# Attention and two MLPs on one core: the row maxima negated two slots at a time, the exponentials one slot later

## The chip, the core and the metric

The kernel runs on one core of a Trainium2 chip. The metric is the time of one execution on the device in microseconds (us). Before the change three runs give a median of 1149.24 us (1142.69 to 1151.27).

The engines that matter here are TensorE (PE, matmuls; PEld is its weight loading), VectorE (DVE), ScalarE (ACT), GpSimd (POOL) and SyncE (SP), which issues the DMAs. Each runs its own instructions in the order of the program, and waits for the others through semaphores.

## The reference

Softmax attention over 4 batches and 12 heads (448 positions, 64 dimensions), with q and k normalized by their root mean square, then two MLPs on 1792 tokens:

```python
q_n, k_n = (rmsnorm(q, g_q), rmsnorm(k, g_k))
scores = scale * np.matmul(q_n, k_n.transpose(0, 1, 3, 2))
scores = scores - np.max(scores, axis=-1, keepdims=True)
attn = np.exp(scores)
attn = attn / (np.sum(attn, axis=-1, keepdims=True) + 1e-09)
attn_out = np.matmul(attn, v)
...
a = x @ w1
b = x @ w2
h = a * b @ w3
x = h @ w_out
...
h = x @ w_in
g = h * np.clip(h + 3.0, 0.0, 6.0) / 6.0
out = g @ w_out
```

## The kernel before

Two heads form a pair, and there are 24 pairs. A pair's scores are made in 8 slots of 112 queries: slot s of pair i is head s // 4, query block s % 4. The main loop of `attention` counts slots t from 0 to 192 and some more. In slot t it emits, in this order:

- `score`: two matmuls (L627, L628) of 112x448 scores into a PSUM bank of the tag "s", of which there are two;
- `expo` of slot t - 1: ACT takes the exponential of the slot in place, with the negated row maximum as its bias, and sums the row (L646; the sum is a second, short ACT instruction);
- `trans` of a pair that began LG = 8 slots earlier: four PE transposes (L653) into a bank of the tag "t", one 128-key block kb of the pair each slot, 7 blocks in 8 slots. Block kb = 0 needs slots 0 to 3 of its pair, block 3 all eight;
- `tlo` of the block of one slot before: DVE takes the low part `xl` (L672);
- `scale_max`: one DVE instruction scales the scores out of the bank into `PP` and takes the row maximum (L634; the maximum comes out through a second, short DVE instruction). Its column of the tile `mx` is column s;
- `negate`: DVE writes minus that maximum to column 8 + s of `mx` (L641), one element per partition;
- `thi`: ACT takes the high part `xh` (L662) of this slot's block, and `pv` multiplies blocks with V (L701, L705, L706, and L687, L693, L696);
- `fill`: work of the first MLP (L252, L391, L396, L88 to L90) with its weight preparation (L148, L149, L151, L338, L340), so that PE has matmuls between the steps of attention;
- tasks that are due in the slot: loads, the splitting of q, k and v into high and low parts (L594, L600, L606, L608, L615, L616), the statistics of q and k (L510, L518, L523 to L553), and the row sums' end (L725, L726), which is due in slot t = 8i + 9 of pair i.

`anchors[t]` keeps the slot's last score matmul, its maximum and the exponential that is emitted in slot t + 1. Filling work of slot t is emitted so that it stands behind the anchors of slot t - 2 or t - 3 on its engine, and some tasks behind those of t - 1 and t.

What stands on each engine is settled by the tile framework's scheduler, which takes the emitted order as priority and puts an instruction ahead of another where its operands come earlier by its own estimate. A changed instruction can therefore move others, on every engine. POOL works in this stage on six kinds of instruction, all with operands in SBUF: the low parts of k, v and x, the low parts of two kinds of weights, and the division by the row sums.

The stage of attention with the first MLP as its filler lasts from about 20 to 600 us. Behind it only matmuls of the second MLP and their weights' preparation run.

## Time and profile before

| | |
|---|---|
| runs, median (lowest to highest) | 1149.24 us (1142.69 to 1151.27) |
| the profiled execution's own time; its span | 1141.81 us; 1140.0 us |
| PE busy | 1103.1 us (97%) |
| DVE busy | 850.8 us (75%), 1927 instructions |
| ACT busy | 812.4 us (71%), 1729 instructions |
| POOL busy | 177.9 us (16%), none of it behind 640 us |
| DMA queue of SP | 76.2% of 16 engines' span |
| granted clock of TensorE, mean | 0.998 |

A busy time is a share of the span and not yet a reason for its length: an engine that is idle costs something only where the engine that sets the end waits for it. So the waits of PE, and the chain of work that ended last, are read beside the busy times.

### The profile page before, as it was taken

The page shows a single profiled execution, that of the slowest core. Times are in us where ns is not written, and L with a number is a line of the kernel's source. Part 1 is how long each engine was busy: PE and PEld are TensorE (multiplying, and loading weights), DVE is VectorE, ACT ScalarE, POOL GpSimd, SP SyncE. Part 2 cuts the span into 40 slices and gives each one's busy share as a digit, 9 for nine tenths or more (in the row PEclk, how much of TensorE's full clock was granted, in tenths as well). Part 3 has the DMA queues.
Part 4 walks back from the last instruction along what each step waited for, and adds up shares of the span by engine and source line. Part 5 has one row for each costly group of instructions (what it writes and reads, how often), then busy time and mean ns, then how long its engine had stood idle before and what let it go on. Part 6 is the DMA issues. An engine that isn't in the chain of part 4 may idle for free.

```text
span 1140.0 us, 17361 instructions
## 1 busy us (share of the span) xinstructions
PE 1103.1 (97%) x5483; PEld 944.0 (83%) x5483; DVE 850.8 (75%) x1927; ACT 812.4 (71%) x1729; POOL 177.9 (16%) x156
## 2 busy tenths in 40 slices
PE   5999999999999999999999999999999999999998
PEld 3545666788887888888888899899989989999998
DVE  5757988779866888778753225999988998887764
ACT  6989778899758878787754433766666776666764
POOL 1133223554322213221102000000000000000000
PEclk9999999999999999999999999999999999999999
DMA  8999655689889988997789998665469955434972
GB/s 267 331 317 342 213 171 164 243 293 377 272 279 316 308 295 269 336 342 253 232 287 324 382 362 299 217 214 200 164 228 362 389 172 168 153 117 160 335 264 74
DMA packets 109660, 299.04 MB, mean 262 GB/s; under 512 B 13280, under 2 KB 46048, under 8 KB 109568
## 3 DMA queue, kind: packets, MB, share of 16 engines
q1 hardware_dynamic: 109568, 297.93, 76.2%
q8 instruction: 43, 0.70, 0.3%
q14 instruction: 49, 0.40, 0.1%
HBM read 230.61 MB, written 67.27 MB: 261 GB/s over the span
## 4 chain that ended last, share of the span: by engine, by line
PE 60%; ACT 7%; DMA 7%; DVE 3%; issue 2%; POOL 0%; SPq 0%; ACTq 0%; POOLq 0%; DVEq 0%
PE acc L1304 17%; PE bank L391 10%; PE sB L1242 8%; PE sA L1242 8%; PE bank L396 5%; DMA rsb<-rsd 2%; PE bank L653 2%; ACT PP L646 1%; PE bank L88 1%; PE bank L89 1%; PE bank L90 1%; PE bank L627 1%; PE bank L628 1%; PE bank L706 1%; DMA raw<-in_wo_dram 1%
## 5 line engine op out<-in xcount | busy, mean ns | idle before, releaser
L1304 PE MATMUL acc<-g,wt 128*128 128x448 f32 x1008 | 211.7, 366 | 1.2 <-ACT g L1192 1.0
L1304 PEld LDWEIGHTS acc<-g,wt 128*128 128x128 f32 x1008 | 188.9, 188 | 17.7 <-ACT g L1192 1.9
L391 PE MATMUL bank<-xhl,ws 128*128 128x448 f32 x768 | 180.5, 367 | 1.6 <-ACT bs L367 1.3
L391 PEld LDWEIGHTS bank<-xhl,ws 128*128 128x128 f32 x768 | 143.5, 188 | 15.1 <-ACT bs L367 1.8
L634 DVE CUSTOM_DVE_ANT_0 PP<-bank,rb,rq 112x448 f32<-112x448 f32 x192 | 128.7, 675 | 27.4 <-PE bank L628 21.1
L646 ACT ACTIVATE PP<-PP,mx 112x448 f32<-112x448 f32 x192 | 127.5, 665 | 28.1 <-DVE mx L641 24.3
L1242 PE MATMUL sA<-xo,wt 128*128 128x448 f32 x504 | 112.0, 366 | 1.1 <-ACT u L1253 1.1
L1242 PE MATMUL sB<-xo,wt 128*128 128x448 f32 x504 | 112.2, 367 | 0.8 <-ACT u L1253 0.6
L252 PE MATMUL bank<-woh,w 128*128 128x384 f32 x256 | 97.6, 509 | 14.6 <-DVE woh L151 10.9
L1242 PEld LDWEIGHTS sB<-xo,wt 128*128 128x128 f32 x504 | 94.4, 188 | 9.9 <-ACT u L1253 1.9
L1242 PEld LDWEIGHTS sA<-xo,wt 128*128 128x128 f32 x504 | 94.6, 188 | 9.6 <-ACT u L1253 1.5
L662 ACT ACTIVATE xh<-bank 128x448 fp32r<-128x448 f32 (+1 forms) x156 | 83.1, 539 | 24.6 <-PE bank L653 20.5
L653 PEld LDWEIGHTS bank<-ident,PP 112*128 112x128 f32 x672 | 78.8, 141 | 23.9 <-issue 6.1
L1011 DVE TENSOR_TENSOR wt<-wf,wt 128x384 fp32r<-128x384 f32 x160 | 87.3, 555 | 15.1 <-ACT wt L1010 14.9
L672 DVE TENSOR_TENSOR xl<-bank,xh 128x448 fp32r<-128x448 f32 x142 | 87.4, 617 | 11.5 <-ACT xh L662 10.1
L653 PE MATMUL bank<-ident,PP 112*128 112x112 f32 x672 | 94.1, 261 | 1.5 <-DVE xl L672 1.1
L396 PE MATMUL bank<-xhl,ws 128*128 128x448 f32 x384 | 94.5, 366 | 0.0
L252 PEld LDWEIGHTS bank<-woh,w 128*128 128x128 f32 x256 | 48.9, 196 | 43.7 <-DVE woh L151 13.4
L148 ACT ACTIVATE raw<-raw 128x384 f32<-128x384 f32 (+1 forms) x112 | 63.8, 569 | 28.6 <-DMA raw<-in_wo_dram 11.6
L1010 ACT ACTIVATE wt<-wf 128x384 fp32r<-128x384 f32 x160 | 80.4, 517 | 4.8 <-PE acc L1304 2.7
L151 DVE SCALAR_TENSOR_TENSOR raw<-raw 128x384 int32<-128x384 int32 x80 | 48.9, 613 | 46.0 <-ACT raw L149 38.8
L627 PE MATMUL bank<-K,Q 128*112 128x448 f32 x192 | 77.7, 407 | 1.5 <-DVE mx L634 1.4
(134 smaller groups left out, 2110.3 us busy)
## 6 DMA issues: line engine op xcount, KB each, us to landing
ws<-w12d SPq DMA_DIRECT2D x48, 768.0 KB, 6.2
ws<-wpd SPq DMA_DIRECT2D x32, 768.0 KB, 6.5
wf<-wfd SPq DMA_DIRECT2D x56, 384.0 KB, 5.6
raw<-in_wo_dram SPq DMA_DIRECT2D x44, 384.0 KB, 5.8
td<-G SPq DMA_DIRECT2D x32, 448.0 KB, 2.5
G<-td SPq DMA_DIRECT2D x32, 448.0 KB, 6.2
raw<-in_w_dram SPq DMA_DIRECT2D x32, 384.0 KB, 6.9
w12d<-ws SPq DMA_DIRECT2D x16, 768.0 KB, 5.9
```

Source lines behind the costliest of these rows:

```text
L252: nc.tensor.matmul(ps[:, :NH], W["w3"][a, c // 4][:, cs], W["woh"][c, n], start=c == 0, stop=c == M1 - 1)
L391: nc.tensor.matmul(ps[:, :S], w[:, 0, ks], x[:, y, :], start=k == 0 and y == 0, stop=False)
L396: nc.tensor.matmul(ps[:, :S], w[:, 1, ks], L["xhl"][i][:, 0, :], start=False, stop=k == KD - 1)
L627: nc.tensor.matmul(ps[:CP, :S], qs, k1[:, j, :], start=True, stop=False)
L634: anchors[8 * i + s].append(nc.vector.tensor_tensor_reduce(out=T["PP", i][:, c, sl], in0=ps[:CP, :S], in1=T["rb", i][:, sl], op0=ALU.mult, ...
L646: anchors[8 * i + s].append(nc.scalar.activation(v, v, AF.Exp, bias=T["m", i][:, 8 + s : 9 + s], accum_out=T["sum", i][:, s : s + 1]))
L653: nc.tensor.transpose(ps[:, c * CP : c * CP + CP], src[:, c, kb * P : kb * P + P], ident[:CP, :CP])
L662: nc.scalar.activation(hi, ps, AF.Copy)
L672: nc.vector.tensor_sub(lo, ps, hi)
L1011: nc.vector.tensor_sub(t[:, 1, :], src, t[:, 0, :])
L1242: mm = nc.tensor.matmul(ps[:, :S], w[:, a, ks], x[:, c, :], start=first and k == 0 and n == 0, stop=k == KD // 2 - 1 and n == 2, skip_grou ...
L1304: nc.tensor.matmul(ps, w[:, y, ns], x[:, z, :], start=first and a == 0, stop=end and a == 2, skip_group_check=h in "674")
```

## The change

The negation is made in every other slot, for two columns of `mx` at once: in an odd slot s it reads columns s - 1 and s and writes columns 7 + s and 8 + s. The exponential of a slot is emitted two slots behind its score instead of one. It is kept in the same place of `anchors` as the exponential that was emitted in that slot before, so the filling work stays behind the exponential of the same loop step. The last exponential is emitted in slot 193 instead of 192.

```diff
@@ score
-            anchors[8 * i + s] = [nc.tensor.matmul(ps[:CP, :S], qs, k2[:, j, :], start=False, stop=True)]
+            anchors.setdefault(8 * i + s, []).append(nc.tensor.matmul(ps[:CP, :S], qs, k2[:, j, :], start=False, stop=True))
@@ negate
-            nc.vector.tensor_scalar_mul(m[:, 8 + s : 9 + s], m[:, s : s + 1], -1.0)
+            nc.vector.tensor_scalar_mul(m[:, 7 + s : 9 + s], m[:, s - 1 : s + 1], -1.0)
@@ expo
-            anchors[8 * i + s].append(nc.scalar.activation(
+            anchors.setdefault(8 * i + s + 1, []).append(nc.scalar.activation(
                 v, v, AF.Exp, bias=T["m", i][:, 8 + s : 9 + s], accum_out=T["sum", i][:, s : s + 1]))
@@ the loop over slots
-            if 0 < t <= 8 * NP:
-                expo(*divmod(t - 1, 8))
+            if 1 < t <= 8 * NP + 1:
+                expo(*divmod(t - 2, 8))
...
-                negate(*divmod(t, 8))
+                if t % 2:
+                    negate(*divmod(t, 8))
```

On DVE, slots 4 and 5 of pair 11 (L634 is a slot's maximum and its short second instruction, L641 the negation, L672 a low part) stood so before:

```order
L634 ISA PP,mx<-bank,rb,rq 112x448
L634 ISA mx 112x1
L672 TENSOR_TENSOR xl<-bank,xh 128x448
L641 TENSOR_SCALAR mx<-mx 112x1
L634 ISA PP,mx<-bank,rb,rq 112x448
L634 ISA mx 112x1
L641 TENSOR_SCALAR mx<-mx 112x1
```

With the change the same two slots stand so (L721 is an addition for an earlier pair):

```order
L634 ISA PP,mx<-bank,rb,rq 112x448
L634 ISA mx 112x1
L721 TENSOR_TENSOR xs<-bank,xs 64x448
L634 ISA PP,mx<-bank,rb,rq 112x448
L634 ISA mx 112x1
L641 TENSOR_SCALAR mx<-mx 112x2
```

The first slot's negation is gone from between the two maxima, and one instruction of two columns stands behind the second maximum.

On ACT, the exponentials of slots 4 to 7 of the same pair (L646) stood so among the copies (L662 is a high part `xh`):

```order
L646 ACTIVATE PP,sum<-PP,mx 112x448
L510 ACTIVATE nat<-nat 112x1024
L646 ACTIVATE PP,sum<-PP,mx 112x448
L662 ACTIVATE xh<-bank 128x448 x2
L606 ACTIVATE K<-kr 128x896
L594 ACTIVATE Q<-qr,gs 128x896
L646 ACTIVATE PP,sum<-PP,mx 112x448
L359 ACTIVATE xhl<-xs 128x448 x2
L372 ACTIVATE abh<-bs 128x448
L646 ACTIVATE PP,sum<-PP,mx 112x448
```

With the change they stand in two pairs:

```order
L646 ACTIVATE PP,sum<-PP,mx 112x448 x2
L662 ACTIVATE xh<-bank 128x448
L372 ACTIVATE abh<-bs 128x448
L606 ACTIVATE K<-kr 128x896
L594 ACTIVATE Q<-qr,gs 128x896
L662 ACTIVATE xh<-bank 128x448
L646 ACTIVATE PP,sum<-PP,mx 112x448 x2
```

Over the whole program 38 of the 191 steps from one exponential to the next had nothing between them on ACT before, and 86 have nothing between them now. DVE has 96 instructions fewer; the counts on the other engines are the same, their order is not.

## Rows read from the trace of the kernel before

**Rows 1.** Windows: busy us (and instructions) by engine, granted clock, DMA share, GB/s.

```profile
core 0: us, PE busy (x) PEld busy (x) DVE busy (x) ACT busy (x) POOL busy (x), PEclk, DMA share, GB/s
20.00:100.00 80.00, 76.25 (x303) 43.48 (x302) 51.88 (x148) 72.58 (x160) 21.22 (x19) 1.00 0.97 321
100.00:220.00 120.00, 115.50 (x555) 83.38 (x554) 102.42 (x273) 100.24 (x227) 45.13 (x39) 1.00 0.63 202
220.00:300.00 80.00, 79.04 (x419) 67.75 (x418) 65.33 (x160) 71.49 (x159) 36.84 (x32) 1.00 0.95 332
300.00:380.00 80.00, 77.19 (x415) 68.06 (x414) 57.47 (x158) 56.28 (x126) 19.13 (x17) 0.98 0.87 290
380.00:580.00 200.00, 196.87 (x1078) 174.79 (x1078) 160.97 (x424) 159.96 (x358) 46.93 (x38) 1.00 0.87 289
```

**Rows 2.** Waits of PE, 20 to 580 us: us in total, times, longest.

```profile
PE bank L705 <- ACT xh L662: 3.5, 5, 1.3
PE bank L696 <- DVE xh L674: 2.4, 1, 2.4
PE bank L252 <- DVE woh L151: 1.5, 1, 1.5
PE bank L252 <- DVE wst L245: 1.5, 1, 1.5
PE bank L627 <- DVE mx L634: 1.4, 4, 0.6
PE bank L391 <- ACT bs L367: 1.3, 1, 1.3
PE bank L653 <- DVE xl L672: 1.1, 5, 0.3
```

**Rows 3.** The page: the chain that ended last, shares of the span by engine.

```profile
PE 60%; ACT 7%; DMA 7%; DVE 3%; issue 2%; POOL 0%; SPq 0%; ACTq 0%; POOLq 0%; DVEq 0%
```

**Rows 4.** The negation's line: duration ns lowest/median/highest; who waited for it.

```profile
L641 DVE TENSOR_SCALAR mx<-mx x192: 130/146/156, 27.4 to 574.1; 112x1 f32<-112x1 f32 x192
  ACT PP L646: 24.3, 27
```

**Rows 5.** Timeline of DVE near 311 us: start us, duration us, instruction.

```profile
311.10 0.15 DVE L641 TENSOR_SCALAR mx<-mx 112x1 f32<-112x1 f32 x1
311.17 0.17 DVE L523 TENSOR_SCALAR ss<-ss 112x32 f32<-112x32 f32 x1
...
312.99 0.14 DVE L641 TENSOR_SCALAR mx<-mx 112x1 f32<-112x1 f32 x1
313.05 0.61 DVE L672 TENSOR_TENSOR xl<-bank,xh 128x448 fp32r<-128x448 f32 x1
```

**Rows 6.** The row sums' line: duration ns lowest/median/highest; below, its group on DVE.

```profile
L725 DVE TENSOR_SCALAR sum<-sum x24: 158/172/1133, 40.4 to 577.5; 112x8 f32<-112x8 f32 x24
L725 DVE TENSOR_SCALAR sum<-sum 112x8 f32<-112x8 f32 x24 | 10.0, 416 | 8.3 <-ACT PP L646 8.1
```

**Rows 7.** Timelines of DVE and of POOL around the longest L725.

```profile
297.88 1.13 DVE L725 TENSOR_SCALAR sum<-sum 112x8 f32<-112x8 f32 x1
299.05 0.20 DVE L726 RECIPROCAL sum<-sum 112x8 f32<-112x8 f32 x1
...
297.42 2.67 POOL L360 TENSOR_TENSOR xhl<-xs,xhl 128x448 fp32r<-128x448 f32 x2
```

**Rows 8.** Timelines of DVE and of POOL around a negation.

```profile
101.69 0.14 DVE L641 TENSOR_SCALAR mx<-mx 112x1 f32<-112x1 f32 x1
101.75 0.61 DVE L672 TENSOR_TENSOR xl<-bank,xh 128x448 fp32r<-128x448 f32 x1
...
100.90 1.10 POOL L227 TENSOR_TENSOR ws<-raw,ws 128x384 fp32r<-128x384 f32 x1 [0.26 <-ACT ws L225]
```

**Rows 9.** Groups of POOL, 20 to 580 us: busy us, mean ns; idle before.

```profile
L608 POOL TENSOR_TENSOR K<-kr,K 128x448 fp32r<-128x448 f32 x48 | 56.2, 1193 | 92.2 <-ACT K L606 84.8 <-PE bank L653 7.3
L340 POOL TENSOR_TENSOR ws<-raw,ws 128x384 fp32r<-128x384 f32 x22 | 23.2, 1063 | 22.7 <-ACT ws L338 19.2 <-DMA w12d<-ws 3.5
```

**Rows 10.** Groups of ACT, 20 to 580 us.

```profile
L646 ACT ACTIVATE PP<-PP,mx 112x448 f32<-112x448 f32 x192 | 127.5, 665 | 28.1 <-DVE mx L641 24.3 <-PE bank L396 2.2 <-PE bank L561 0.9
L662 ACT ACTIVATE xh<-bank 128x448 fp32r<-128x448 f32 (+1 forms) x148 | 78.9, 539 | 24.6 <-PE bank L653 20.5 <-PE bank L561 2.9
L646 ACT ACTIVATION_READ_ACCUMULATOR PP<-PP,mx 112x1 f32 x192 | 37.2, 194 | 0.0
```

## The prediction

> **What bounds the kernel now.** I read the windows first, because the change touches one stage alone. From 20 to 580 us PE is busy 76.25 + 115.50 + 79.04 + 77.19 + 196.87 = 544.85 of 560 us [rows 1]: it is idle for 15.2 us. DVE is busy there 51.88 + 102.42 + 65.33 + 57.47 + 160.97 = 438.1 us (78%), ACT 460.6 us (82%). So PE sets the end, and DVE and ACT matter where PE waits for them. The waits of PE come next [rows 2]: those that DVE ended among the rows shown are 2.4 + 1.5 + 1.5 + 1.4 + 1.1 = 7.9 us, those that ACT ended 3.5 + 1.3 = 4.8 us. That is 12.7 us which quicker DVE and ACT could give back; the rest of the span is matmuls that nobody removes. Third, the chain of work that ended last [rows 3]: DVE holds 3% of it, some 34 of 1140 us against 850.8 us that it is busy, so about 4% of a microsecond of DVE work reaches the end; ACT holds 7%, some 80 us of 812.4, about 10%. I use these two shares as the price of a microsecond on either engine.
>
> **The change part by part.** *96 negations go.* Each lasts 0.146 us [rows 4], but DVE starts its next instruction 0.06 to 0.07 us after the negation's start [rows 5]. So DVE gains 96 x 0.06 = 5.8 us; the other bound is the whole duration, 96 x 0.146 = 14.0 us. I take 5.8, because the next start is what the next instruction sees.
>
> *96 negations become two columns wide.* The nearest wider row of the same operation is L725 with 8 columns, at least 0.158 us [rows 6]: at most 0.012 us each, 1.2 us; at least nothing. I take 1.2.
>
> *The wider form may wait for POOL.* The negation of one column never lasts over 0.156 us, in 192 instances, POOL at work or not [rows 4]: at 101.69 us it lies inside a POOL instruction (100.90 to 102.00) and takes 0.14 [rows 8]. L725 is the same kind of DVE instruction with 8 columns, from SBUF to SBUF: its median is 0.172 us and its longest 1.133, and its mean 0.416 [rows 6]. The longest starts at 297.88, when POOL has been at work for 0.46 us, and ends at 299.01; POOL's two instructions from 297.42 take 2.67 us, so the first ends near 298.8 to 298.9 [rows 7]. It stood until POOL's first instruction was over. Two columns could behave as one, or as eight. If as eight: POOL is busy for 21.22 + 45.13 + 36.84 + 19.13 + 46.93 = 169.3 of the 560 us, 30% [rows 1], and its instructions last about 1.2 us [rows 9], so 96 x 0.30 = 29 negations meet one and wait for half of it, 0.6 us: 17.4 us. The bounds are nothing (as one column), and 96 times L725's mean over its median, 96 x (0.416 - 0.172) = 23.4 us. I take 17.4: the operation, its memory and its type are L725's, and only one column has been seen to be exempt.
>
> The Trainium skill speaks against the change here: *Vector Engine (DVE) Microarchitecture Reference*, section 5.1 (performance modes), says that a one-source instruction on two elements per partition in SBUF runs in the mode that uses both ports, and *SBUF — State Buffer*, "Who interferes with whom", that such an instruction and a GpSimd one exclude each other, whichever starts first holding the ports for all of its time. By that rule the 17.4 us stand; by the rows of the one-column form alone they would be 0. That two elements are enough is shown by no row of before.
>
> What is queued behind such a wait is DVE's next instruction, mostly a maximum (L634) or a low part (L672). For these wait PE's next scores (1.4 us in 4 waits now) and transposes (1.1 us in 5) [rows 2], and the two exponentials on ACT wait for the negation itself.
>
> DVE in sum: -5.8 + 1.2 + 17.4 = +12.8 us. At 4% that is +0.5 us at the end.
>
> *The exponentials move a slot.* Each issues two ACT instructions, 0.665 and 0.194 us, and no DMA [rows 10]. ACT now idles 24.3 us, 27 times, for the negation [rows 4]. An odd slot's exponential now has its bias ready one slot earlier; an even one waits for the pair's negation, which its slot's successor makes, as close behind as before. So I let half of that idle time go: -12.2 us of ACT, at 10% -1.2 us. What is late next is what stands behind two adjacent exponentials: 86 - 38 = 48 more adjacent pairs in the order push a following copy by 0.665 us. PE waited 5 times among 148 copies `xh` [rows 2, 10], 3.4%: 48 x 0.034 x 0.665 = +1.1 us.
>
> *The row sums (L725) come due in slot 9 of their pair; the exponential of slot 7 now is emitted in that slot instead of the one before.* DVE waits 8.1 us for these exponentials now [rows 6]. If it doubles, DVE loses 8 us, at 4% +0.3 us. The bound is 24 x (0.665 + 0.194) = 20.6 us, +0.8. The transposes of key block 3 need that exponential in slot 11; two slots of cover remain, at some 2.9 us a slot (560 us for 192). Were the cover gone, ACT's 0.86 us would stand in front of PE 24 times, 20.6 us.
>
> *The order of the other instructions moves on every engine, SP's loads among them.* No row prices that. The instructions and bytes are the same; between 20 and 100 us the DMA share is 0.97 [rows 1], where a load that is issued later can't be caught up. I take 0, with a few us both ways.
>
> **The sum.** +0.5 - 1.2 + 1.1 + 0.3 = +0.7 us on the profiled execution's 1141.8: 1142.5. That execution lies 7.4 us below the median 1149.24 and just below the lowest run shown, 1142.69. The runs of a changed kernel may fall at either level, so I choose the middle and add half of the 7.4: **1146 us**.
>
> **The rivals.**
>
> *Slower: the POOL waits sit in PE's path.* Place: DVE's queue between a pair's second maximum and the next score bank. For it: L725 shows waits of up to 0.97 us over its median, and the scores already wait for maxima [rows 2, 6]. Against it: DVE has 122 idle us in the stretch to absorb them [rows 1], and PE has filling matmuls between scores. If all 29 waits reach PE, +17.4 us: 1159 on the profiled scale, 1163 on the forecast's. It decides slower by over 1% from about 20 of the 29 on (20 x 0.6 = 12 us). The two sections of the Trainium skill named above state the rule behind this rival.
>
> *Faster: two columns don't wait for POOL, and the pairs free ACT.* Then DVE gains 4.6 to 14.0 us, ACT 12.2 us or more, and the waits of PE shrink: at most the 12.7 us of rows 2, so 1129 on the profiled scale and 1133 on the forecast's. For it: half the biases are ready early. Against it: it needs nearly all of PE's waits gone, one of which (2.4 us, L696) has nothing to do with maxima.
>
> *Nothing but the order's shuffle.* The negations' time and waits stay off PE's path entirely, and only the new order shows, +/- 6 us: 1140 to 1152. For it: PE is 97% busy over 560 us. Against it: the change pairs the exponentials all through the stage, which the shuffle alone would not.
>
> **How the numbers follow.** Forecast 0.50, slower 0.19, faster 0.15, shuffle alone 0.16. One per cent is 11.5 us, and about what a measurement of this kernel can tell from no change (its three runs spread 8.6 us). Forecast and shuffle lie within it: 0.66. The range leaves out about one in ten at each end: low 1134, at nearly the faster rival's 1133, and high 1160, some way into the slower one. The likeliest case's own range is 1140 to 1152.
>
> **What the profile after would show.** Line L641: 96 instances; if the POOL term is right, its median stays near 0.15 us and its longest is near 1 us, its mean near 0.3; if it stays below 0.17 throughout, that term is nothing. L646's wait for L641 falls from 24.3 to near 12 us. L725's wait for L646 rises to near 16 us. PE's waits for `xh` rise by about a microsecond, and PE's idle time from 20 to 580 us stays between 12 and 20 us. The prediction is wrong if PE's idle time grows past 25 us with waits on L634 or L641 in front (the slower rival), if it falls below 6 (the faster one), or if PE waits for a load that it did not wait for before.

## The result, and the profile after

The changed kernel takes 1159.3 us (median of 12 runs, 1154.38 to 1166.84), the kernel before beside it 1144.66 us (12 runs, 1140.87 to 1153.41). The ratio is 1.0122, with a 95% interval of [1.0097, 1.0147]: slower by 1.2%, some 14 us (the medians differ by 14.6). The forecast was 1146 us, and that the change would stay within 1% either way. The time lies inside the range of 1134 to 1160 us, at its upper end; that the kernel would not get slower was wrong.

The profiled execution of the changed kernel took 1162.23 us (before: 1141.81), so the two traces differ by more than the medians, 20.5 us of span. The stages after the change, which answer to [rows 1] (columns: busy us and instructions by engine, granted clock of TensorE, DMA share, GB/s):

```profile
core 0: us, PE busy (x) PEld busy (x) DVE busy (x) ACT busy (x) POOL busy (x), PEclk, DMA share, GB/s
20.00:100.00 80.00, 75.35 (x286) 42.09 (x285) 51.21 (x126) 69.59 (x154) 21.13 (x18) 0.96 0.92 304
100.00:220.00 120.00, 113.88 (x524) 80.65 (x523) 101.85 (x250) 97.18 (x220) 40.23 (x35) 0.97 0.64 208
220.00:300.00 80.00, 79.50 (x418) 70.00 (x419) 62.59 (x141) 68.62 (x156) 36.18 (x32) 0.98 0.87 300
300.00:380.00 80.00, 76.86 (x408) 66.41 (x407) 55.69 (x136) 57.06 (x129) 23.04 (x19) 0.98 0.91 294
380.00:580.00 200.00, 190.18 (x1022) 166.79 (x1021) 164.55 (x376) 152.88 (x340) 46.51 (x38) 0.98 0.85 281
```

Two things are to be seen. PE is busy for 535.8 of the 560 us, so it is idle for 24.2 us instead of 15.2. And the granted clock is below 1.00 in every stage, where before it was so in one. In these stages PE does 112 matmuls fewer (2658 against the 2770 of [rows 1], where a matmul at a border counts in both rows); they are left for the time after 580 us.

The mean granted clock of the whole span, before and after (columns: span, clock):

```profile
core 0: 1140.0 us, clock 0.998
```

```profile
core 0: 1160.5 us, clock 0.988
```

A clock of 0.988 over 1160.5 us is 13.9 us of full-speed time not granted, one of 0.998 over 1140.0 us 2.3 us. So the two traces differ by 11.6 us for the clock and by 9.1 us for PE's idle time between 20 and 580 us. Together that is 20.7, and the spans differ by 20.5. The whole span agrees: the same 5483 matmuls keep PE busy for 1115.3 us instead of 1103.1, 12.2 us longer, and PE is idle for 45.2 us instead of 36.9.

These are two single executions, and a pair that lies far apart. Each run on record carries its granted clock. Over the 12 runs of the change it is 0.985 to 0.994, on average 10.3 us of full-speed time not granted; over the 125 runs of the kernel before that were taken beside the experiments it is 0.991 to 1.000, on average 3.7 us. So the clock stands for some 6.6 of the 14 us, about half, and PE's idle time for about the other half.

The waits of PE from 20 to 580 us after the change, which answer to [rows 2] (columns: us in total, times, longest):

```profile
PE bank L705 <- ACT xh L662: 7.2, 7, 1.9
PE bank L627 <- DVE mx L634: 4.3, 8, 1.2
PE bank L696 <- DVE xh L674: 3.5, 3, 1.8
PE bank L391 <- ACT bs L367: 2.5, 1, 2.5
PE bank L252 <- DVE woh L151: 1.8, 1, 1.8
PE bank L88 <- ACT bs L412: 1.7, 1, 1.7
PE bank L701 <- ACT xh L662: 1.4, 1, 1.4
```

ACT ends 7.2 + 2.5 + 1.7 + 1.4 = 12.8 us of these, against 3.5 + 1.3 = 4.8 us of the rows shown before; most of the growth is copies `xh` (7.2 + 1.4 against 3.5). The wait of the next scores for a maximum (L627 for L634) also grew, from 1.4 to 4.3 us. The chain that ended last, by engine, answers to [rows 3]; it still has 7% of ACT, and 5% of DVE instead of 3%:

```profile
PE 74%; DMA 10%; ACT 7%; DVE 5%; issue 2%; SPq 1%; POOL 0%; ACTq 0%; DVEq 0%; POOLq 0%
```

The negation's line (duration ns lowest/median/highest, then who waited for it), its group on DVE (busy us, mean ns), and the row sums' group (the last figure is DVE's wait for L646), which answer to [rows 4, 6]:

```profile
L641 DVE TENSOR_SCALAR mx<-mx x96: 146/168/1214, 28.4 to 595.3; 112x2 f32<-112x2 f32 x96
  ACT PP L646: 21.3, 18
```

```profile
L641 DVE TENSOR_SCALAR mx<-mx 112x2 f32<-112x2 f32 x96 | 30.2, 314 | 1.1
L725 DVE TENSOR_SCALAR sum<-sum 112x8 f32<-112x8 f32 x24 | 5.2, 216 | 15.2 <-ACT PP L646 15.2
```

The negation of two columns does wait for POOL: its longest is 1.214 us, its mean 0.314. The one below starts while a POOL row of two instructions is at work (timelines of DVE and of POOL: start us, duration us):

```profile
213.74 1.13 DVE L641 TENSOR_SCALAR mx<-mx 112x2 f32<-112x2 f32 x1
214.79 0.18 DVE L545 TENSOR_TENSOR rt<-rt,ss 112x32 f32<-112x32 f32 x1
```

```profile
213.69 2.30 POOL L608 TENSOR_TENSOR K<-kr,K 128x448 fp32r<-128x448 f32 x2 [3.53 <-ACT K L606]
```

What the forecast didn't have is a place such as this, at 361 us. ACT after the change (timeline: start us, duration us, instruction, and in brackets the idle time before it):

```profile
357.30 0.54 ACT L412 ACTIVATE bs<-bank 128x448 f32<-128x448 f32 x1
357.74 0.66 ACT L646 ACTIVATE PP<-PP,mx 112x448 f32<-112x448 f32 x1
358.30 0.19 ACT L646 ACTIVATION_READ_ACCUMULATOR PP<-PP,mx 112x1 f32 x1
358.40 0.66 ACT L646 ACTIVATE PP<-PP,mx 112x448 f32<-112x448 f32 x1
358.95 0.19 ACT L646 ACTIVATION_READ_ACCUMULATOR PP<-PP,mx 112x1 f32 x1
359.42 0.54 ACT L148 ACTIVATE raw<-raw 128x384 f32<-128x384 f32 x1 [0.27 <-DMA raw<-in_win_dram]
359.86 0.52 ACT L149 ACTIVATE raw<-raw 128x384 int32<-128x384 uint16 x1
360.29 0.52 ACT L662 ACTIVATE xh<-bank 128x448 fp32r<-128x448 f32 x1
```

PE there (the same columns), and the granted clock around it (columns as in the stages above):

```profile
358.73 0.57 PE L653 MATMUL bank<-ident,PP 112*128 112x112 f32 x4 [0.28 <-DVE xl L675]
359.08 0.45 PE L696 MATMUL bank<-xl,vo 128*128 128x448 f32 x1
360.87 0.57 PE L705 MATMUL bank<-xh,vo 128*128 128x448 f32 x1 [1.34 <-ACT xh L662]
361.52 1.01 PE L653 MATMUL bank<-ident,PP 112*128 112x112 f32 x4
```

```profile
357.00:361.00 4.00, 1.89 (x10) 0.97 (x8) 1.77 (x5) 3.71 (x10) 1.12 (x2) 1.00 1.05 335
361.20:364.40 3.20, 3.12 (x14) 2.48 (x13) 2.83 (x7) 1.67 (x4) 0.00 (x0) 0.50 1.02 396
364.60:368.00 3.40, 3.40 (x19) 3.06 (x18) 3.27 (x9) 0.55 (x1) 0.00 (x0) 1.00 1.04 327
```

Two exponentials stand back to back on ACT, from 357.74 to 359.14, then two conversions of weights, and only then the copy `xh` for which PE waits 1.34 us. The pair is not what set this copy's start, though: ACT stood idle for 0.27 us ahead of the first conversion, until its load had landed, so by the profile that conversion, and the copy behind it, would have started no earlier with one exponential fewer in front. The order on ACT made this copy late; that the pair did is not shown here. After a stretch in which PE was busy for 1.89 of 4 us, the granted clock falls to 0.50 (1.2 GHz) for the next 3.2 us shown, and four transposes take 1.01 us at 361.52 instead of 0.57 at 358.73. Such stretches at half clock stand at eight places ahead of 700 us in this trace, and at one in the trace before (350.4 us). Of PE's waits in the 4 us ahead of each of the eight, the longest was ended by ACT at four (125.6, 221.1, 361.1 and 484.0 us) and by DVE at the other four.

### The profile page after: what moved, and what is told of

Same layout as the page of the kernel before. It is cut to its first block, busy times and chain, and to the rows that moved or that the text cites. A ratio compares the mean times of both kernels' runs of the same rounds, so it can differ in the third digit from the quotient of the medians.

```text
span 1160.5 us, 17275 instructions
## 1 busy us (share of the span) xinstructions
PE 1115.3 (96%) x5483; PEld 951.2 (82%) x5483; DVE 865.2 (75%) x1831; ACT 812.2 (70%) x1729; POOL 179.0 (15%) x156
## 4 chain that ended last, share of the span: by engine, by line
PE 74%; DMA 10%; ACT 7%; DVE 5%; issue 2%; SPq 1%; POOL 0%; ACTq 0%; DVEq 0%; POOLq 0%
PE acc L1305 17%; PE bank L391 11%; PE sB L1243 8%; PE sA L1243 8%; PE bank L396 5%; PE bank L252 5%; PE bank L653 4%; PE bank L90 2%; PE bank L89 2%; PE bank L88 2%; DMA raw<-in_wo_dram 2%; PE bank L627 2%; DMA nat<-in_nat_dram 2%; PE bank L628 2%; PE bank L705 2%
## 5 line engine op out<-in xcount | busy, mean ns | idle before, releaser
L391 PE MATMUL bank<-xhl,ws 128*128 128x448 f32 x768 | 182.1, 372 | 2.7 <-ACT bs L367 2.5
L634 DVE CUSTOM_DVE_ANT_0 PP<-bank,rb,rq 112x448 f32<-112x448 f32 x192 | 128.6, 676 | 27.3 <-PE bank L628 21.7
L646 ACT ACTIVATE PP<-PP,mx 112x448 f32<-112x448 f32 x192 | 126.7, 665 | 27.3 <-DVE mx L641 21.3
L672 DVE TENSOR_TENSOR xl<-bank,xh 128x448 fp32r<-128x448 f32 x142 | 87.3, 618 | 22.8 <-ACT xh L662 21.5
L662 ACT ACTIVATE xh<-bank 128x448 fp32r<-128x448 f32 (+1 forms) x156 | 82.9, 539 | 23.1 <-PE bank L653 21.2
L396 PE MATMUL bank<-xhl,ws 128*128 128x448 f32 x384 | 96.9, 368 | 0.0
L252 PEld LDWEIGHTS bank<-woh,w 128*128 128x128 f32 x256 | 49.9, 201 | 45.0 <-DVE woh L151 13.7
L627 PE MATMUL bank<-K,Q 128*112 128x448 f32 x192 | 78.8, 412 | 4.7 <-DVE mx L634 4.3
L151 DVE SCALAR_TENSOR_TENSOR raw<-raw 128x384 int32<-128x384 int32 x80 | 51.4, 644 | 40.4 <-ACT raw L149 30.8
```

The lines of the kernel that those rows point to most:

```text
L252: nc.tensor.matmul(ps[:, :NH], W["w3"][a, c // 4][:, cs], W["woh"][c, n], start=c == 0, stop=c == M1 - 1)
L391: nc.tensor.matmul(ps[:, :S], w[:, 0, ks], x[:, y, :], start=k == 0 and y == 0, stop=False)
L396: nc.tensor.matmul(ps[:, :S], w[:, 1, ks], L["xhl"][i][:, 0, :], start=False, stop=k == KD - 1)
L627: nc.tensor.matmul(ps[:CP, :S], qs, k1[:, j, :], start=True, stop=False)
L634: anchors[8 * i + s].append(nc.vector.tensor_tensor_reduce(out=T["PP", i][:, c, sl], in0=ps[:CP, :S], in1=T["rb", i][:, sl], op0=ALU.mult, ...
L646: anchors.setdefault(8 * i + s + 1, []).append(nc.scalar.activation(v, v, AF.Exp, bias=T["m", i][:, 8 + s : 9 + s], accum_out=T["sum", i][ ...
```

## The experiments

Four theories stand in the expectations. **A**: the two-column negation waits for POOL, and these waits reach PE (the slower rival). **B**: a negation taken once for two slots lets both exponentials start at the same time; they stand back to back on ACT, and ACT's copies behind them come late for PE, with half-clock stretches after PE's pauses. **C**: the loss is one unlucky order out of many that the scheduler could have found. **D**: standing back to back does no harm; the even slot's exponential is simply late, since its negation waits for the next slot's maximum.

"Pairs" are exponentials that follow each other directly in ACT's order, out of 191 neighbours: 38 before, 86 after the change. All ratios are to the kernel before, run beside each kernel. "Idle" is PE's idle time from 20 to 580 us and "clock" the mean granted clock, both of one profiled execution. "Not granted" is the span times what its mean clock lacks of 1, averaged over all runs of the kernel; the profiled execution of e12 has the highest clock of its 12 runs, that of e16 the lowest.

| run | negation | exponentials | pairs | ratio, 95% interval | idle us | clock | not granted, us |
|---|---|---|---|---|---|---|---|
| before | one column | one slot behind | 38 | 1 | 15.1 | 0.998 | 3.7 |
| the change | two columns | two slots | 86 | 1.0122 [1.0097, 1.0147] | 24.2 | 0.988 | 10.3 |
| e3 | two, by reduction | two slots | 86 | 1.0104 [1.0067, 1.0142] | 20.6 | 0.990 | 8.9 |
| e5 | two, by reduction | two slots, looser filling | 87 | 1.0066 [1.0040, 1.0092] | 22.4 | 0.993 | 6.3 |
| e10 | two, by reduction | both in one even slot | 93 | 1.0204 [1.0158, 1.0250] | 29.2 | 0.990 | 11.1 |
| e7 | two, by reduction | odd ones behind `xh` | 29 | 1.0035 [1.0014, 1.0055] | 16.4 | 0.997 | 5.5 |
| e13 | two columns | odd ones behind `xh` | 29 | 1.0017 [0.9993, 1.0042] | 16.1 | 0.995 | 4.6 |
| e16 | two columns | all behind `xh` | 24 | 1.0052 [1.0025, 1.0079] | 16.8 | 0.989 | 8.2 |
| e1 | one, in odd slots | two slots | 43 | 1.0023 [0.9990, 1.0057] | 23.7 | 0.994 | 6.9 |
| e2 | one column | two slots | 43 | 1.0037 [1.0006, 1.0067] | 17.5 | 0.993 | 8.6 |
| e17 | one column | two slots, all behind `xh` | 24 | 1.0016 [0.9987, 1.0045] | 14.6 | 0.994 | 7.7 |
| e12 | one, in odd slots | even behind odd | 92 | 1.0040 [1.0012, 1.0067] | 21.1 | 0.997 | 6.7 |
| e15 | one, in odd slots | as e12, one slot earlier | 93 | 1.0088 [1.0058, 1.0118] | 26.1 | 0.991 | 11.7 |
| e4 | two columns, each slot | one slot | 38 | 1.0057 [1.0027, 1.0086] | 17.9 | 0.994 | 5.9 |
| e14 | one column | one slot, all behind `xh` | 24 | 0.9906 [0.9867, 0.9944] | 12.0 | 0.995 | 4.4 |
| e18 | one column | one slot, odd behind `xh` | 13 | 0.9943 [0.9915, 0.9972] | 13.7 | 0.996 | 4.7 |
| e19 | one column | one slot, `xh` behind them | 35 | 1.0001 [0.9971, 1.0030] | 18.4 | 0.997 | 4.9 |
| e20 | as the change | other filling (1.35) | 86 | 1.0109 [1.0075, 1.0144] | 23.2 | 0.994 | 9.2 |
| e21 | as before | other filling (1.35) | 35 | 1.0039 [1.0015, 1.0064] | 17.3 | 0.997 | 6.0 |
| e22 | as the change | other filling (1.25) | 85 | 1.0099 [1.0063, 1.0135] | 20.0 | 0.994 | 8.7 |

### The wait for POOL alone, and the parts of the change alone

**e3, the change without a wait for POOL.** A reduction over one element takes the negative of both maxima; every engine's order is that of the changed kernel.

```diff
-            nc.vector.tensor_scalar_mul(m[:, 7 + s : 9 + s], m[:, s - 1 : s + 1], -1.0)
+            nc.vector.tensor_reduce(m[:, 7 + s : 9 + s], m[:, s - 1 : s + 1].unsqueeze(2), axis=AX.X, op=ALU.max, negate=True)
```

> The changed kernel, with the pair's negation made by one reduction (a maximum over one element, its sign flipped) instead of the multiplication by -1. It is still one DVE instruction of two columns, and the order of instructions on every engine is that of the changed kernel. Theory A (the two-column multiplication waits for POOL, and what stands behind it on DVE and ACT makes PE wait): no negation lasts over 0.2 us, L646 waits for L641 near 12 us instead of 21.3, and the time falls back to that of the kernel before, ratio 0.99 to 1.003. Theory B (two exponentials next to each other, one slot later, hold ACT up) and theory C (the new order itself is worse): as the changed kernel, ratio 1.009 to 1.015.

1158.06 us, 1.0104. Its negations no longer wait (duration ns lowest/median/highest, and who waited for the line):

```profile
L641 DVE TENSOR_REDUCE mx<-mx x96: 131/148/156, 27.0 to 587.9; 112x2 f32<-112x2 f32 x96
  ACT PP L646: 16.1, 14
```

The wait is gone wholly and the loss stays almost wholly: 1.0104 against 1.0122. By these figures A carries some 0.2%; their intervals alone would allow it up to about half of the loss. The next scores' wait for a maximum stays as well (3.8 us, against 4.3 in the change), though no negation waits any more.

**e2, the exponentials two slots behind and nothing else** (a one-column negation in each slot), and **e1, two one-column negations in the odd slot**, so that neither exponential can start before the odd slot but no wide instruction is there.

```diff
-                if t % 2:
-                    negate(*divmod(t, 8))
+                negate(*divmod(t, 8))        # e2, with the one-column form of before
```

```diff
-            nc.vector.tensor_scalar_mul(m[:, 7 + s : 9 + s], m[:, s - 1 : s + 1], -1.0)
+            [nc.vector.tensor_scalar_mul(m[:, 8 + z : 9 + z], m[:, z : z + 1], -1.0) for z in (s - 1, s)]
```

> The exponentials stand two slots behind their scores, but each slot's maximum is negated by its own one-column instruction in its slot, as before. Theory A: no wait for POOL, so as the kernel before, ratio 0.99 to 1.005. Theory B: the lateness of the exponentials is kept, ratio 1.005 to 1.015. Theory C: another order again, anything from 0.995 to 1.015.

> The changed kernel, with the pair's negation made by two one-column instructions, one behind the other, in the odd slot. Theory A: no wait for POOL, ratio 0.99 to 1.005. Theory B: exponentials in pairs and late, ratio 1.005 to 1.015. Theory C: another order, and the difference between this one and the one with the lag alone (which does the same work) says how much an order is worth: up to 0.01.

1148.44 us, 1.0037, and 1147.57 us, 1.0023: the further slot costs 0.2 to 0.4%, and the interval of e1 reaches down to nothing. Both are misses for B, which wanted 1.005 or more from the lateness it shares with the change, and lie where A had them. In e1 the scheduler moved most of the even slots' negations ahead again, so only 43 pairs came about, and e1 is no more than a second order of e2.

**e4, wide negations in the order of before.** Each slot's negation is made two columns wide in place, eight columns apart, the second one holding zeros (24 short memsets are added, and the exponential takes its bias from the first column), so 192 instructions can wait for POOL.

```diff
-            nc.vector.tensor_scalar_mul(m[:, 8 + s : 9 + s], m[:, s : s + 1], -1.0)
+            nc.vector.tensor_scalar_mul(m[:, s : 9 + s : 8], m[:, s : 9 + s : 8], -1.0)
```

> The kernel before, with each slot's negation widened to two columns (the second one is not used; its columns are cleared once a pair by a small DVE memset, 24 in all). Exponentials, their lag and ACT's order stay as before. There are 192 two-column multiplications instead of 96. Theory A: their mean is near 0.3 us, they add near 30 us to DVE, twice the changed kernel's 14, and the ratio is 1.010 to 1.03. Theories B and C: as the kernel before, ratio 0.998 to 1.005, though the negations last longer.

1151.91 us, 1.0057. L641 has a median of 0.163 and a mean of 0.281 us here: 192 x 0.118 = 23 us of waits, and 6.7 us of time over the 1145.24 of before. For the change's 96 that would be half, 0.3%. It lies below what A wanted (1.010 or more) and above what B and C did (at most 1.005). With e3 (0.2%) and e13 below (less than nothing against e7) the wait for POOL is worth 0 to 0.3% of the 1.2, an estimate, since each of these differences is as large as its interval.

### The pairs

**e7, the reduction, but the two exponentials of a pair kept apart.** The odd slot's exponential is queued on ACT behind the last copy `xh`. **e13** does the same with the changed kernel's own two-column multiplication, **e16** puts every exponential of the changed kernel behind the last `xh`.

```diff
+            es = ExitStack()
+            if s % 2 and "hi" in T:          # e16: without "s % 2"
+                es.enter_context(tc.issue_after(T["hi"].ins))
+            with es:
             anchors.setdefault(8 * i + s + 1, []).append(nc.scalar.activation(
...
-                nc.scalar.activation(hi, ps, AF.Copy)
+                T["hi"] = nc.scalar.activation(hi, ps, AF.Copy)
```

> The pair's negation by one reduction (no wait for POOL), and the exponential of each odd slot must stand behind the copy xh of the slot before on ACT: 29 of 191 steps from one exponential to the next have nothing between them, against 86 in the changed kernel and 38 in the kernel before. Theory B (two adjacent exponentials hold up the copies that PE waits for): back to the kernel before, ratio 0.997 to 1.004. Theory D (adjacency is harmless; the even slot's exponential and all that is placed behind it come later because its negation waits for the next slot's maximum): as with the reduction alone, ratio 1.007 to 1.014. Theory C (the order that the scheduler happened to find): any ratio from 0.997 to 1.015.

> The changed kernel's two-column multiplication, but the odd slot's exponential stands behind a copy xh, so 29 pairs are left back to back (86 in the changed kernel). Same order as the run with the reduction apart (1.0035). Theory A: the wait for GpSimd makes most of the loss, ratio 1.010 or more. Theory B: the wait is worth 0.2 to 0.3%, so 1.005 to 1.007. L641 should show a mean near 0.31 us again, with a longest over 1 us.

> The changed kernel (negation taken once for two slots by the two-column multiplication, exponentials two slots behind) with one rule added: each exponential is queued on ScalarE behind the last copy xh issued before it. 24 pairs back to back (86 without the rule). Theory B (back-to-back exponentials hold up the copies): the whole loss goes, 0.990 to 1.001, as with the kernel before under the same rule (0.9906). Theory A (wait for GpSimd in the two-column negation): the loss stays, 1.010 or more. Theory C (chance of the order): anywhere from 0.995 to 1.012.

1.0035, 1.0017 and 1.0052: with 24 to 29 pairs instead of 86, each of the three is 0.7 to 1.05% quicker than its like with 86 pairs (e7 than e3, e13 and e16 than the change), and PE's idle time falls to between 16.1 and 16.8 us. In all three the even slot's negation still waits for the next slot's maximum, so D's 1.007 to 1.014 for e7 isn't met. But the rule isn't neutral: on the kernel before it gains 0.6 to 0.9% as well (e18 and e14 below), so what e7, e13 and e16 gain is not yet the price of the pairs. A fails again: e13 waits for POOL as the change does (mean 0.324 us) and is no slower than e7, which doesn't. B foresaw less than was left in e16 (0.990 to 1.001) and more than was left in e13 (1.005 to 1.007). The PE waits of e16 show what took the place (us in total, times, longest; the copy is L666 here, the low part L676):

```profile
PE bank L709 <- ACT xh L666: 3.1, 3, 1.7
PE bank L710 <- DVE xl L676: 3.1, 4, 1.9
PE bank L657 <- DVE xl L676: 2.3, 5, 0.8
```

**e10, more of it.** The reduction, with both exponentials of a pair issued in the same even slot.

```diff
-            if 1 < t <= 8 * NP + 1:
+            if t and t % 2 == 0 and t <= 8 * NP:
                 expo(*divmod(t - 2, 8))
+                expo(*divmod(t - 1, 8))
```

> The pair's negation by one reduction, and both exponentials of a pair emitted in the slot behind it: the odd slot's exponential is one slot behind its score as before, the even slot's two. 93 adjacent exponentials. Theories B and D: as with the reduction alone, ratio 1.006 to 1.014, since the lag of the odd slots is not the cause. If the lag of one slot is what costs: ratio 0.997 to 1.004. Theory C: any ratio.

1169.78 us, 1.0204, the slowest of all, with 93 pairs, and beyond the 1.014 that B and D allowed. PE's waits for `xh` are 12.9 us, against the change's 7.2 + 1.4:

```profile
PE bank L705 <- ACT xh L662: 12.9, 14, 2.7
```

**e5, another order with as many pairs** (the filling work of a slot is tied to the exponential of one slot earlier, which holds it back less).

```diff
-            anchors.setdefault(8 * i + s + 1, []).append(nc.scalar.activation(
+            anchors.setdefault(8 * i + s + 2, []).append(nc.scalar.activation(
```

> The pair's negation by one reduction, and the filling work of the first MLP may stand behind an exponential of one slot earlier (the exponential is kept one place later in the slots' anchors): another order on PE, ACT, DVE and SP with the same work and 87 adjacent exponentials. Theories B and D: ratio 1.006 to 1.014 again. Theory C (one unlucky order): away from 1.010, between 0.997 and 1.006.

1153.91 us, 1.0066 with 87 pairs: slower than before, and less so than e3, its like (1.0104), though the two intervals meet. That the particular order counts as well is likely, not shown.

**e12 and e15, pairs without a two-column instruction.** The work is that of e1; the even slot's exponential is queued on ACT behind the odd slot's. In e15 both are issued a slot earlier, as in e10.

```diff
+            if s % 2 == 0:
+                es.enter_context(tc.issue_after(T["odd"].ins))
...
-            if 1 < t <= 8 * NP + 1:
+            if 1 < t <= 8 * NP + 1 and t % 2:          # e15: t % 2 == 0, t - 1 and t - 2
                 expo(*divmod(t - 2, 8))
+                expo(*divmod(t - 3, 8))
```

> Work of the kernel before (two negations of one column each, no two-column instruction, so no wait of VectorE for GpSimd in L641), exponentials two slots behind, but the even slot's exponential is queued on ScalarE behind the odd slot's, one after the other in 92 of 96 pairs (86 in the changed kernel). Theory A (wait for GpSimd in the two-column negation): nothing of it is left, ratio 1.000 to 1.004 as in the other narrow kernels. Theory B (two exponentials back to back hold up ScalarE's copies that TensorE waits for, and each pause is followed by a stretch at half clock): 1.008 to 1.014, with 10 us or more at half clock before 700 us. Theory C (the particular order found by the scheduler): anything from 1.002 to 1.02, not tied to the count of pairs.

> As the narrow kernel with the even slot's exponential queued behind the odd slot's, but both are issued one slot earlier, as in the reduction without the second slot of lag (93 pairs there, 1.0204). 93 pairs here, two one-column negations. Theory A: 1.000 to 1.004. Theory B: 1.008 to 1.02, close to the reduction's 1.0204, since only the negation's instruction differs. Theory C: 1.002 to 1.02.

1.0040 and 1.0088. e15 shows B without any wide negation, and its wait is again the copy:

```profile
PE bank L710 <- ACT xh L667: 11.8, 8, 2.7
```

e12 is a miss for B, which wanted 1.008 or more, and lies just where A had it. Yet it has the waits that B speaks of; the rows of PE's waits for ACT:

```profile
PE bank L710 <- ACT xh L667: 6.2, 5, 1.8
...
PE bank L391 <- ACT bs L367: 1.9, 1, 1.9
PE bank L88 <- ACT bs L412: 1.6, 1, 1.6
PE bank L698 <- ACT xh L667: 1.4, 1, 1.4
```

That is 11.1 us, close to the change's 12.8. The profiled clock is 0.997 here and 0.988 in the change, but this is e12's highest; over all runs e12 has 6.7 us not granted, between the 3.7 of before and the change's 10.3. Against e1 and e2 (1.0023 and 1.0037 with 43 pairs), which have one-column negations and the further slot too, the 92 pairs of e12 cost 0.0 to 0.2%, less than the intervals can tell.

### Is it the change or the draw?

**e14, e18, e19: the kernel before with other rules for ACT's order.** In e14 each exponential is queued behind the last `xh`, in e18 the odd ones only (the lines of e7 on the kernel before), in e19 the copies behind the last exponential. **e17** is e2 with the rule of e14.

```diff
-                nc.scalar.activation(hi, ps, AF.Copy)
+                with tc.issue_after(T["ex"].ins):          # e19
+                    nc.scalar.activation(hi, ps, AF.Copy)
```

> The kernel before, with every exponential queued behind the last copy xh on ScalarE: 24 pairs back to back instead of 38, one negation per slot, one slot behind as before. Theory B: the fewer pairs, the better; ratio 0.997 to 1.000. Theory C: any new order of the same work lies within 0.996 to 1.006 of the kernel before, and says nothing on pairs.

> The kernel before, with the rule on the odd slots' exponentials alone. 13 pairs back to back (38 in the kernel before, 24 with the rule on all). Theory B by the count of pairs: 0.985 to 0.995. If what counts is that no exponential stands ahead of a copy that is ready, not the pairs: 0.993 to 1.000, about half of the gain of the rule on all. Theory C: 0.996 to 1.006.

> The kernel before with the opposite rule: each copy xh is queued on ScalarE behind the exponential issued before it, so a copy that is ready early can no longer pass an exponential. 35 pairs back to back (38 before), so by pairs alone nothing changes: 0.997 to 1.003. If what counts is that a copy xh stands behind an exponential: 1.003 to 1.015, with more waits of TensorE for xh. Theory C: 0.996 to 1.006.

> One negation of one column a slot as before, exponentials two slots behind as in the change, and each exponential queued behind the last copy xh. 24 pairs. Without the rule it was 1.0037 with 43 pairs. Theory B: 0.988 to 0.998, close to the kernel before under the same rule. Theory C: 0.995 to 1.006.

e14 is faster than both kernels: 1133.56 us, 0.9906 [0.9867, 0.9944]. PE is idle for 12.0 us there, and of its waits for `xh` only these are left among the longest:

```profile
PE bank L709 <- ACT xh L666: 1.4, 3, 0.7
PE bank L705 <- ACT xh L666: 0.7, 1, 0.7
```

Both theories that spoke on e14 had it higher (B at 0.997 or more, C at 0.996 or more). e18 gains 0.57%, less than e14, although it has fewer pairs (13 against 24): the number of pairs alone doesn't set the time. e19, with the opposite rule and about the old number of pairs, changes nothing (1.0001). e17 stays at 1.0016: with exponentials two slots behind, the rule brings back at most what the further slot costs (e2: 1.0037), where B wanted 0.988 to 0.998, and against e14 the further slot costs 1.1%.

These runs also give the comparison that the pairs need: kernels under the same rule, with the same 24 pairs. The kernel before is then at 0.9906 (e14), with the exponentials two slots behind at 1.0016 (e17), and with the whole change at 1.0052 (e16). With the pairs made equal the change still costs 1.0052 / 0.9906 = 1.015, no less than the 1.012 without the rule, and most of it comes with the further slot. By the rule on odd slots it is 1.0017 / 0.9943 = 1.007 (e13 to e18, with 29 and 13 pairs). So the loss does not go away with the pairs, and lateness of the exponentials, which D blames, stands as a rival again. Without the rule the further slot alone cost at most 0.4% (e2), so no theory of the four fits all runs.

**e20, e21, e22: other draws of the order.** One number that has nothing to do with the change, the filling work per slot at the start, is 1.35 or 1.25 us instead of 1.3. That gives other orders on every engine.

```diff
-            return 1.3, 3
+            return 1.35, 3          # e22: 1.25
```

> The changed kernel with 1.35 us of filling work a slot instead of 1.3 while no pool of it is open: another order on every engine, 86 pairs back to back as in the changed kernel. Theory B (the loss belongs to the change): 1.008 to 1.016 against the kernel before. Theory C (the loss is one bad draw of the order): 0.997 to 1.006.

> The changed kernel with 1.25 instead of 1.3: a third order of the change, 85 pairs. Theory B: 1.008 to 1.016. Theory C: 0.997 to 1.008.

> The kernel before with the same 1.35: another order on every engine, 35 pairs (38 before). It gives the scatter of orders by itself. Theory B: 0.996 to 1.004, and the ratio of the changed kernel with 1.35 to this one 1.006 or more. Theory C: anywhere from 0.994 to 1.008, and that ratio anywhere about 1.

The change comes out at 1.0109 and 1.0099 in two further orders, after 1.0122 in its own, and the kernel before at 1.0039 in one. So the loss belongs to the change, and C as its cause falls; what C describes is a scatter of some 0.4% here. The ratio of e20 to e21, which have the same filling, is 1156.8 / 1149.07 = 1.0067, the low end of what B wanted.

What PE waits for is not the same in these orders. In e22 its waits for the copies are shorter than before the change, and those for maxima are longer (its four longest rows):

```profile
PE bank L627 <- DVE mx L634: 7.0, 9, 1.7
PE bank L653 <- DVE xl L672: 2.4, 7, 0.8
PE bank L391 <- ACT ws L338: 2.2, 1, 2.2
PE bank L705 <- ACT xh L662: 1.8, 4, 1.2
```

So late copies `xh` are a part of the loss in the change's own order and in e10 and e15, and no part of it in e22, which loses 0.99% all the same.

Over all kernels, the eight with 85 pairs or more have ratios of 1.0040 to 1.0204, on average 1.0104; the twelve with 43 or fewer, the kernel before among them, 0.9906 to 1.0057, on average 1.0010. The two groups differ in more than the pairs: six of the eight have the joint negation and none has the rule, while ten of the twelve have the rule or exponentials one slot behind.

## Why the prediction was wrong, point by point

**What held.** The change removes 96 negations and makes 96 wait for POOL, as the term of 17.4 us said: 96 x (0.314 - 0.168) = 14.0 us were measured. A two-column negation lasts up to 1.214 us, a one-column one at most 0.156 [rows 4]. The Trainium skill (*SBUF — State Buffer*, "Who interferes with whom") states that a VectorE instruction that uses both ports and a GpSimd one exclude each other; two elements per partition behave by that rule here. DVE's busy time rose from 850.8 to 865.2 us, by 14.4 where the sum gave 12.8. At 4% that was +0.5 us, 0.04%; e3, e7 against e13, and e4 put the waits at 0 to 0.3%: small, as was forecast, though the 4% itself is not confirmed. The row sums wait 15.2 us for their exponentials, where near 16 was forecast. So the slower rival's time (1159 to 1163 us) came true, but not by its mechanism: e3, whose negations don't wait for POOL, has the loss as well.

**The step that failed: "48 x 0.034 x 0.665 = +1.1 us", what PE waits for late copies on ACT.** In the trace after, PE's waits for `xh` rose from 3.5 to 8.6 us and its waits for ACT in the rows shown by 8.0 us. The 3.4% was the share of all copies that PE waited for before, and that share is no constant: it belongs to the order and to the lag in which the copies stand. Nor is a pair's 0.665 us the delay of a copy: behind the exponentials stand conversions of weights and `bs` sums that the scheduler put in front of `xh`, some of them with a wait for a load, as at 361 us above. The term's own mechanism, copies made late by back-to-back exponentials, is borne out in part only. In the trace after, 11 pauses of PE longer than 0.3 us between 20 and 640 us are ended by an instruction of ACT, and in 8 of them two exponentials stand back to back among the eight ACT instructions ahead of it; before it was none of 8. But of all 207 copies into `xh` and `bs` in that stretch 98 have such a pair ahead, so some 5 of the 11 were to be expected by chance. And e16 keeps the loss against e14 with the same 24 pairs. Which part of the change makes PE wait longer, the pairs, the further slot or the order that came with them, stays open.

**The terms that weren't there: waits for maxima, and the clock.** The sum priced DVE's work at 4% and found +0.5 us; PE's waits for maxima alone (L627 for L634) rose from 1.4 to 4.3 us, and stand at 3.8 in e3, where no negation waits for POOL. The price came from [rows 3], whose shares add up to 79% of the span only. And the sum priced waits at their length, without a term for the clock. In the trace, pauses such as the 1.34 us at 360.87 are followed by a stretch at 1.2 GHz, and 11.6 of the 20.5 us between the two traces are clock, some 6.6 of the 14 us over all runs. The four transposes at 361.52 take 1.8 times as long as those at 358.73. The Trainium skill (*TensorE: Matmul & The Clock Gate*, "Terms") takes the cost of throttled time as that time times the share of pulses left out; here that is half. PE's busy time agrees: it is 12.2 us longer for the same matmuls, and the clock accounts for 11.6. The profile before showed one such place as 0.98 in [rows 1], and the prediction passed over it. Clock and idle time together give the spans of e20 (4.6 + 8.1 of 12.9 us) and e22 (4.6 + 4.9 of 9.7) to within the rounding of the clock, 0.6 us, but neither e14's (its span is 8.7 us below that of before at a lower clock) nor those of e2 and e4, so this is an account of single traces and no law. Nor does the time not granted follow the pairs: it is 8.6 us in e2 with 43 of them, 6.7 in e12 with 92 and 8.2 in e16 with 24.

**"I let half of that idle time go: -12.2 us of ACT."** It fell from 24.3 to 21.3 us only, in 18 waits instead of 27: each is longer (1.18 us against 0.90), most likely since an even slot's exponential waits through the next slot. At the same 10% the term is -0.3 us, not -1.2.

**"The order of the other instructions: I take 0, with a few us both ways."** Fair: e21 and e19 lie at 1.0039 and 1.0001. What was left out beside it is that the further slot itself costs something: e1, e2 and e17 lie at 1.0016 to 1.0037, up to 4 us, and e17 against e14 at 1.1%, some 13 us.

**The level.** 3.7 us were added for the low place of the profiled execution; the 12 runs of before have their median 2.9 us above it. That step held, and the forecast stood for a ratio of 1146 / 1144.66 = 1.001.

**The bounds.** "The prediction is wrong if PE's idle time grows past 25 us with waits on L634 or L641 in front": it grew to 24.2, past the 12 to 20 that were foreseen and close to this bound, with `xh` first and L634 second. (A slip beside it: the longest L725 lies 0.96 us over its median, not 0.97.)

**In sum**, of the 1.2%: the wait for POOL is worth 0 to 0.3 (an estimate), an unlucky order is not the cause (three orders of the change lie at 1.0099 to 1.0122), and about half of the time is clock, the rest mostly PE's waits. The further slot alone costs 0.2 to 0.4, or 1.1 under the rule of e14. That the pairing makes the rest is argued, not shown: e7, e13 and e16 give back 0.7 to 1.05, but the rule by which they do it gives the kernel before 0.6 to 0.9 as well.

**What stays open.** B, the pairs, met its range in e3, e5, e7, e15, e18, e19, e20, e21 and e22, and missed it in e1, e2, e4, e10, e12, e13, e14, e16 and e17. e12 has the pairs and nearly the change's waits for ACT at 1.0040, and e15 (1.0088) costs less than half of e10 (1.0204) with the same pairs: something in taking both negatives with one instruction may cost beyond the pairs and POOL, in orders that differ on every engine, and no run separates it. A kernel with the change's lag and order and only its pairs taken apart was not made. Nor is it explained why e14's span is 8.7 us shorter than that of before: PE is idle for 3.3 us less over the whole span, and the same 5483 matmuls keep it busy for 5.4 us less (1097.7 against 1103.1), although its clock is lower.

## What to carry to other kernels

A change that takes out small instructions can move long ones. Here the 96 merged negations release two exponentials each at the same moment and later than before, and the order on every engine is built anew around them; so price what stands behind them on each engine in the order that was built, and not by an average share of waits. On a kernel whose PE is 97% busy, look at the granted clock of each stage too, in several runs, for a pause can cost more than its length. Before a rule that undoes part of a change is taken as the price of that part, try the rule on the kernel before: here keeping each exponential behind the copy that PE waits for gave 0.9% there, without any of the change.

## What the runs showed of the hardware

A negation of two columns waits for POOL (mean 0.314 us, longest 1.214), a one-column one does not (longest 0.156 in 192), and neither does the reduction of two columns with the negative taken in it (longest 0.156 in 96 in e3).

The granted clock fell to 0.50 in the midst of a stage in which PE is 96% busy: ahead of 361.2 us PE had been busy for 1.89 of 4 us, with a wait of 1.34 us as the longest shown, and it then worked at 1.2 GHz for the 3.2 us of the middle row before the clock was back at 1.00. A forecast that prices only the waits misses such stretches.
